# A shorter formula for g when h is small, with the long one in a second program behind a bound

## Chip, core and metric

The kernel runs on one NeuronCore of a Trainium2 chip. The metric is the device time of one execution in microseconds (us); the lower the better. Names of engines: PE is TensorE (matmuls), ACT is ScalarE, DVE is VectorE, POOL is GpSimd, SP is SyncE, which issues most DMAs.

## What is computed

Attention with a sigmoid in place of the softmax, and behind it a two-layer product with the function h - tanh(h) between the layers. Shapes: 8 batches, 12 heads, 448 tokens, 64 columns a head; the layers are 768 x 2048 and 2048 x 768.

```python
scores = scale * np.matmul(q, k.transpose(0, 1, 3, 2)) - np.log(S)
attn = 1.0 / (1.0 + np.exp(-scores))
x = np.matmul(attn, v)            # then (B*S, H*D)
h = x @ w_in
g = h - np.tanh(h)
out = g @ w_out
```

With the reference's own inputs h is small: its largest magnitude is 0.0230, worked out from them.

## The kernel before

All work goes batch by batch, 448 tokens each. A batch has an attention part (scores, `weigh` for the sigmoid, `split_a`, `av`), a first product `moe1` (x by w_in, into `ph`) and a second, `moe2` (g by w_out, into `po`, and `por` for the last 64 tokens). Numbers that need more than 16 bits are split into a high and a low half of 16 bits (`parts`, `split`, `halves`), and a product then takes three matmuls. While PE does the second product of batch b, ACT and DVE do the attention of batch b + 1, whose matmuls stand among those of the product; so PE has one unbroken queue. In batch 0 there is no batch before it: there the weights are loaded and split among the rest, and the first product is done in 32 bits (line 999 of the page).

`mix` makes g from h. It is called once for each pair of 128 columns of h, 8 times a batch, 64 times in all, on a tile of 128 partitions x 896 values (two halves of 448 tokens). Before, it computes two things: a polynomial m in u = h² (two Squares with biases on ACT, two products on DVE), good for small h, and th = h - tanh(h) (Tanh on ACT, one subtraction on DVE), good for large h. A Relu of u - 0.65² on ACT is zero or not, and `copy_predicated` on DVE (line 845) puts th in place of m where it isn't. `halves` splits the result into the two 16-bit halves of `g`, one on ACT (line 780) and one on DVE (line 781), a pair later (`finish_g`).

The order on PE, ACT, DVE and POOL is the order in which the code is written (`manual_schedule`). In batch 0 a string, `ORDER`, spells it out, letter by letter: `M` is half a pair of the first product, `t` the next step of the generator `mix`, `P` a step of the second product, `B` a block of the attention of batch 1, `A` and `a` a split of w_out, `C` a step of the loading of w_out. A `t` whose generator has ended does nothing. In the batches after it, `mix` runs behind each pair in `moe1`; its last call of a batch is carried out during the second product, at the steps named in `TAIL` (1, 2, 3, 4, 5), where a step is six matmuls of 384 columns.

Four kinds of PSUM tiles are shared: `sc` (two buffers: scores, `ph`), `mm` (two: `po`), `av` and `tr` (one each: sums of the attention, transposes). A matmul into one waits until the last reader of the tile before has ended. So `mix` holds `ph` until the last of its instructions that reads it.

Of the kernel before, what the change touches and what calls it, by code (L numbers as in the profile page):

```python
# [10 lines left out]
F32 = mybir.dt.float32  # L11
# [3 lines left out]
AF = mybir.ActivationFunctionType  # L15
ALU = mybir.AluOpType
AX = mybir.AxisListType
PSUM = bass.MemoryType.PSUM

P = 128  # L20
# [4 lines left out]
CUT = 0.65  # L25

KAPPA = 0.00592396
B1, C1 = 0.62576354, 2.54375998**2  # L30
# [1 line left out]


class Builder:

    AV32 = 2

# [23 lines left out]
    def __init__(self, ctx, tc, q, k, v, w_in, w_out, out):  # L61
        self.tc, self.nc = tc, tc.nc
        self.q, self.k, self.v, self.w_in, self.w_out, self.out = q, k, v, w_in, w_out, out
        self.B, self.NP, _, self.S = q.shape
        self.DM, self.DFF = w_in.shape
        self.NC = self.DM // P
        self.NF = self.DFF // P
        self.HALF = self.DM // 2
        nc = self.nc
        pool = lambda name, bufs, **kw: ctx.enter_context(tc.tile_pool(name=name, bufs=bufs, **kw))  # L70
        self.const = pool("const", 1)
        self.wp = pool("weights", 1)
        self.sm = pool("small", 2)
        self.nat = pool("nat", 2)
        self.qk = pool("qk", 2)
        self.att = pool("att", 2)
        self.xp = pool("xp", 8)
        self.tp = pool("temps", self.TP)
        self.op = pool("outs", 2)
        self.ps = pool("ps", 1, space=PSUM)  # L80

        self.ident = self.const.tile([P, P], F32, name="ident")
        make_identity(nc, self.ident)
        self.rows = self.const.tile([P, D], BF16, name="rows")
        nc.vector.tensor_tensor(self.rows, self.ident[:, 0::2], self.ident[:, 1::2], op=ALU.add)
        self.onesf = self.const.tile([P, P], F32, name="onesf")
        nc.vector.memset(self.onesf, 1.0)
        self.onesb = self.const.tile([P, P], BF16, name="onesb")
        nc.vector.memset(self.onesb, 1.0)

        self.NB = self.DFF // 256
        self.wi = self.wp.tile([P, self.NC * self.NB + self.SHIFT, 2, 256], F16, name="wi")
        self.wo = self.wp.tile([P, self.NF * 2 + self.SHIFT_O, 2, self.HALF], F16, name="wo")
# [628 lines left out]
    def h_scales(self, ix):  # L722

        V = self.nc.vector
        t1 = lambda name: self.sm.tile([P, 1], F32, name=name)
        ih, ihk = t1("ih"), t1("ihk")
        V.tensor_tensor(ih, ix, self.iSwi, op=ALU.mult)
        V.tensor_scalar(ihk, ih, KAPPA, None, op0=ALU.mult)
        return ih, ihk

    def split_x(self, hl, x, Sx, act):
# [89 lines left out]
    def mix(self, ps, g, ih, ihk):  # L821

        nc = self.nc
        V = nc.vector
        temp = lambda name: self.tp.tile([P, 2, self.S], F32, name=name, tag="t")
        u = temp("u")
        nc.scalar.activation(u, ps, AF.Square, scale=ih)  # L827
        th = temp("th")
        nc.scalar.activation(th, ps, AF.Tanh, scale=ih)  # L829
        m = temp("m")  # L830
        V.scalar_tensor_tensor(m, ps, ihk, u, op0=ALU.mult, op1=ALU.mult)  # L831
        V.scalar_tensor_tensor(th, ps, ih, th, op0=ALU.mult, op1=ALU.subtract)  # L832
        yield 1
        self.finish_g()
        yield 1
        q1 = temp("q1")
        nc.scalar.activation(q1, u, AF.Square, bias=self.b1)  # L837
        V.scalar_tensor_tensor(m, q1, C1, m, op0=ALU.add, op1=ALU.mult)  # L838
        yield 1
        q2 = temp("q2")  # L840
        nc.scalar.activation(q2, u, AF.Square, bias=self.b2)  # L841
        V.scalar_tensor_tensor(m, q2, C2, m, op0=ALU.add, op1=ALU.mult)  # L842
        yield 1
        nc.scalar.activation(u, u, AF.Relu, bias=self.b3)  # L844
        V.copy_predicated(m, u.bitcast(U32), th)  # L845
        yield 1
        self.late.append((m, g))
# [88 lines left out]
    def build(self):  # L936
        nc, tc = self.nc, self.tc

        def const(name, value, n=1):
            t = self.const.tile([P, n], F32, name=name)  # L940
            nc.vector.memset(t, value)
            return t

        self.nls = const("nls", -math.log(self.S))
        self.b1 = const("b1", B1)
        self.b2 = const("b2", B2)
        self.b3 = const("b3", -CUT * CUT)
        self.tiny = const("tiny", TINY)
        self.ih0 = const("ih0", 1.0)
        self.ihk0 = const("ihk0", KAPPA)  # L950
        self.iSwo = const("iswo", 1.0, 3)
        self.sums = [const(f"ss{i}", 0.0, 6) for i in range(2)]
        self.Swo = []
        self.sums_out, self.bound = [[], []], [None, None]
        self.xs32, self.x2b = False, []
        pieces = list(self.pieces())
        nA = 4 * self.NC
        E = mybir.EngineType
        with tc.manual_schedule(engines={E.PE, E.Activation, E.DVE, E.Pool}):
            nB = nA + self.NF + self.EARLY  # L960
            self.stage = tc.alloc_tile_pool(name="stage", bufs=2, reuse_waits="tile")
            self.blocks = self.stream()
            self.first(
                self.convert(pieces[:nA], "attention"),
                self.convert(pieces[nA:nB], "mixture"),
                self.convert(pieces[nB:], "product"),
            )
        with tc.manual_schedule(engines={E.PE, E.Activation, E.DVE, E.Pool, E.SP}):
            for b in range(1, self.B):
                self.batch(b)  # L970
        self.gp.release()
# [148 lines left out]
        assert not events  # L1120


def build_kernel(tc, q, k, v, moe_w_in, moe_w_out, out):
    with ExitStack() as ctx:
        Builder(ctx, tc, q, k, v, moe_w_in, moe_w_out, out).build()


# [27 lines left out]
```

## Time and profile before

| | |
|---|---|
| device time, median of 3 runs | 1165.98 us (1165.82 to 1166.71) |
| profiled execution, span from first to last instruction | 1164.3 us |
| PE, busy with matmuls | 1152.6 us, 99% of the span, 7585 matmuls |
| DVE | 904.5 us, 78% |
| ACT | 863.5 us, 74% |
| POOL | 77.9 us, 7% |
| PE's granted clock | 0.999 of full speed |

Of the profiled execution the page tells its span and no other time; the median lies 1.7 us over it, which is what stands around the first and last instruction. An engine's share is an average over stages. What one stage is worth is read from the stretches, and from what an engine waited for in each. The records of PE's matmuls overlap, since they are pipelined: a record is longer than the distance from one to the next.

### The profile page before, as it was taken

The page shows a single profiled execution, that of the slowest core. Times are in us where ns is not written, and L with a number is a line of the kernel's source. Part 1 is how long each engine was busy: PE and PEld are TensorE (multiplying, and loading weights), DVE is VectorE, ACT ScalarE, POOL GpSimd, SP SyncE. Part 2 cuts the span into 40 slices and gives each one's busy share as a digit, 9 for nine tenths or more (in the row PEclk, how much of TensorE's full clock was granted, in tenths as well). Part 3 has the DMA queues.
Part 4 walks back from the last instruction along what each step waited for, and adds up shares of the span by engine and source line. Part 5 has one row for each costly group of instructions (what it writes and reads, how often), then busy time and mean ns, then how long its engine had stood idle before and what let it go on. Part 6 is the DMA issues. An engine that isn't in the chain of part 4 may idle for free.

```text
span 1164.3 us, 18920 instructions
## 1 busy us (share of the span) xinstructions
PE 1152.6 (99%) x7585; PEld 601.2 (52%) x7585; DVE 904.5 (78%) x1294; ACT 863.5 (74%) x1185; POOL 77.9 (7%) x58
## 2 busy tenths in 40 slices
PE   9999999999999999999999999999999999999998
PEld 2355444555555555555555555555555555555565
DVE  6999998699866996679857897778976798646930
ACT  7998986589976888768887688867887688745820
POOL 0000000000220002100021000300022000300000
PEclk9999999999999999999999999999999999999999
DMA  9942171000321002210022100210012100000000
GB/s 358 360 161 72 45 219 54 22 8 1 88 78 60 1 1 77 62 53 1 17 75 62 40 1 31 87 58 19 1 60 80 53 1 10 22 28 8 1 15 34
DMA packets 34056, 70.43 MB, mean 60 GB/s; under 512 B 3888, under 2 KB 21040, under 8 KB 33968
## 3 DMA queue, kind: packets, MB, share of 16 engines
q1 hardware_dynamic: 33744, 68.89, 18.1%
q8 instruction: 59, 0.97, 0.3%
q10 hardware_dynamic: 224, 0.33, 0.1%
q14 instruction: 29, 0.24, 0.1%
HBM read 58.20 MB, written 11.01 MB: 59 GB/s over the span
## 4 chain that ended last, share of the span: by engine, by line
PE 88%; DVE 5%; ACT 3%; DMA 3%; issue 1%; DVEq 0%; ACTq 0%; SPq 0%
PE ph L787 33%; PE po L873 30%; PE acc L434 8%; PE sc L403 8%; PE por L921 5%; PE ph L999 3%; DMA raw<-moe_w_in 2%; DVE wo L250 1%; ACT a L414 1%; DMA qnn<-q 1%; DVE g L781 0%; DVE wo L249 0%; PE nm L704 0%; DVE m L845 0%; PE wl L204 0%
## 5 line engine op out<-in xcount | busy, mean ns | idle before, releaser
L873 PE MATMUL po<-wo,g 128*128 128x384 f16 x2304 | 388.7, 326 | 1.9 <-DVE wo L250 1.0
L787 PE MATMUL ph<-xhl,wi 128*128 128x448 f16 x2016 | 382.6, 352 | 0.0
L873 PEld LDWEIGHTS <-g 128*128 128x128 f16 x2304 | 220.6, 98 | 167.1 <-issue 23.5
L787 PEld LDWEIGHTS <-wi 128*128 128x128 f16 x2016 | 196.7, 98 | 185.0 <-issue 2.1
L421 DVE SCALAR_TENSOR_TENSOR ahl<-a,ahl 128x896 f16<-128x896 f32 x126 | 161.5, 1317 | 127.0 <-ACT ahl L420 126.9
L414 ACT ACTIVATE a<-sc,nls,rn 128x896 f32<-128x896 f32 x147 | 155.8, 1090 | 40.8 <-PE sc L403 39.4
L827 ACT ACTIVATE u<-ph,ih 128x896 f32<-128x896 f32 x64 | 64.4, 1006 | 72.3 <-PE ph L787 70.7
L420 ACT ACTIVATE ahl<-a 128x896 f16<-128x896 f32 x126 | 113.2, 940 | 0.6
L403 PE MATMUL sc<-Q,K 64*128 64x448 f16 x1008 | 100.8, 353 | 2.0 <-DVE th L832 1.3
L780 ACT ACTIVATE g<-m,Sg 128x896 f16<-128x896 f32 x64 | 66.6, 1041 | 36.6 <-DVE m L845 30.3
L831 DVE SCALAR_TENSOR_TENSOR m<-ph,ihk,u 128x896 f32<-128x896 f32 x64 | 73.4, 1147 | 24.1 <-ACT th L829 23.8
L845 DVE COPY_PREDICATED m<-u,th 128x896 f32<-128x896 uint32 x64 | 77.3, 1208 | 7.1 <-ACT u L844 0.8
L434 PE MATMUL acc<-ahl,vhl 128*64 128x448 f16 (+1 forms) x864 | 80.6, 356 | 0.0
L781 DVE SCALAR_TENSOR_TENSOR g<-m,Sg,g 128x896 f16<-128x896 f32 x64 | 73.3, 1146 | 6.7 <-ACT g L780 6.7
L465 POOL TENSOR_TENSOR x<-x 128x448 f32<-128x448 f32 x24 | 27.1, 1128 | 763.9 <-ACT x L448 763.9
L842 DVE SCALAR_TENSOR_TENSOR m<-q,m 128x896 f32<-128x896 f32 x64 | 69.8, 1091 | 6.8 <-DVE m L838 0.5
L999 PE MATMUL ph<-x,wi 128*128 128x448 f32 x192 | 74.1, 540 | 0.0
L832 DVE SCALAR_TENSOR_TENSOR th<-ph,ih,th 128x896 f32<-128x896 f32 x64 | 73.2, 1144 | 0.0
L838 DVE SCALAR_TENSOR_TENSOR m<-q,m 128x896 f32<-128x896 f32 x64 | 69.5, 1086 | 0.0
L844 ACT ACTIVATE u<-u,b 128x896 f32<-128x896 f32 x64 | 66.7, 1042 | 1.9
L837 ACT ACTIVATE q<-u,b 128x896 f32<-128x896 f32 x64 | 65.8, 1028 | 0.0
L841 ACT ACTIVATE q<-u,b 128x896 f32<-128x896 f32 x64 | 65.8, 1028 | 0.0
(142 smaller groups left out, 1086.3 us busy)
## 6 DMA issues: line engine op xcount, KB each, us to landing
knn<-k SPq DMA_DIRECT2D x45, 224.0 KB, 2.6
qnn<-q SPq DMA_DIRECT2D x44, 224.0 KB, 2.6
rawo<-moe_w_out SPq DMA_DIRECT2D x22, 384.0 KB, 5.6
out<-o SPq DMA_DIRECT2D x21, 384.0 KB, 2.3
raw<-moe_w_in SPq DMA_DIRECT2D x13, 512.0 KB, 8.1
vn<-v SPq DMA_DIRECT2D x24, 256.0 KB, 2.8
wo<-moe_w_in SPq DMA_DIRECT2D x11, 512.0 KB, 8.3
vn<-v SPq DMA_DIRECT2D x24, 192.0 KB, 2.4
```

What stands on the lines that cost most here:

```text
L403: self.nc.tensor.matmul(ps[i * m : (i + 1) * m, h, : self.S], K[i][r, w, c * P : c * P + m], Q[i][r, x, :], start=(n == 0), stop=(n == len ...
L414: self.nc.scalar.activation(a[:, 0], ps[:, :, : self.S], AF.Sigmoid, bias=self.nls, scale=scale)
L420: nc.scalar.activation(A[:, 0], a[:, 0], AF.Copy, scale=A_SCALE)
L421: nc.vector.scalar_tensor_tensor(A[:, 1], a[:, 0], A_SCALE, A[:, 0], op0=ALU.mult, op1=ALU.subtract)
L434: self.nc.tensor.matmul(acc[i][h * D : (h + 1) * D, : self.S], v[k, w, 2 * QT + h if half else h * QT + c], A[k, x, h], start=(n == 0 and ...
L781: nc.vector.scalar_tensor_tensor(g[:, 1], m, Sg, g[:, 0], op0=ALU.mult, op1=ALU.subtract)
L787: self.nc.tensor.matmul(ph, self.wi[:, self.slot(c, k), part, e * P : (e + 1) * P], xhl[c][:, x, :], start=(i == 0), stop=(i == len(prods) ...
L831: V.scalar_tensor_tensor(m, ps, ihk, u, op0=ALU.mult, op1=ALU.mult)
L832: V.scalar_tensor_tensor(th, ps, ih, th, op0=ALU.mult, op1=ALU.subtract)
L845: V.copy_predicated(m, u.bitcast(U32), th)
L873: nc.tensor.matmul(po[i][:, :H], gs[f // 2][:, x, f % 2, tk * P : (tk + 1) * P], self.wo[:, i * self.NF + 2 * ks[f // 2] + f % 2, w], star ...
L999: nc.tensor.matmul(ph[:, e, :S], self.fp32(self.wi, self.slot(c, k))[:, 0, e * P : (e + 1) * P], xs[c], start=(c == 0), stop=(c == self.NC ...
```

## The change

A class `Small` takes the place of `Builder`, with another `mix`. It has the polynomial alone, of one degree less: u = h² (ACT), m = h·u·κ (DVE), one Square with a bias (ACT), one product (DVE); no tanh, no Relu, no predicated copy, and three steps in place of five. A `tensor_reduce` keeps the largest u of each partition in one column of `squares` for each pair. After the last pair of the last batch, `largest` reduces these columns, transposes them on PE and reduces again, to one number in `flag`. Behind the whole program each engine loads the flag into a register and compares it with 0x3D7FFFFF (the bits of the float just under 0.0625, that is |h| = 0.25). Above it, the kernel of before runs, complete, and writes the output again.

```diff
+SMALL_BITS = 0x3D7FFFFF
+KAPPA_S = 0.051974997
+B_S, C_S = -1.2822222, 4.7692432
...
-        V.tensor_scalar(ihk, ih, KAPPA, None, op0=ALU.mult)
+        V.tensor_scalar(ihk, ih, self.KAPPA, None, op0=ALU.mult)
...
+class Small(Builder):
+    KAPPA = KAPPA_S
+
+    def __init__(self, ctx, tc, flag, *args):
+        super().__init__(ctx, tc, *args)
+        V = self.nc.vector
+        self.flag = flag
+        self.squares = self.const.tile([P, self.B * self.NB], F32, name="squares")
+        V.memset(self.squares, 0.0)
+        self.bs = self.const.tile([P, 1], F32, name="bs")
+        V.memset(self.bs, B_S)
+        self.seen = 0
+
+    def mix(self, ps, g, ih, ihk):
+        nc = self.nc
+        V = nc.vector
+        temp = lambda name: self.tp.tile([P, 2, self.S], F32, name=name, tag="t")
+        u = temp("u")
+        n, self.seen = self.seen, self.seen + 1
+        nc.scalar.activation(u, ps, AF.Square, scale=ih)
+        m = temp("m")
+        V.scalar_tensor_tensor(m, ps, ihk, u, op0=ALU.mult, op1=ALU.mult)
+        yield 1
+        self.finish_g()
+        yield 1
+        q = temp("q")
+        nc.scalar.activation(q, u, AF.Square, bias=self.bs)
+        V.scalar_tensor_tensor(m, q, C_S, m, op0=ALU.add, op1=ALU.mult)
+        V.tensor_reduce(self.squares[:, n : n + 1], u, axis=AX.XY, op=ALU.max)
+        if self.seen == self.B * self.NB:
+            self.largest()
+        yield 1
+        self.late.append((m, g))
+
+    def largest(self):
+        nc = self.nc
+        m = self.sm.tile([P, 1], F32, name="largest")
+        nc.vector.tensor_reduce(m, self.squares, axis=AX.X, op=ALU.max)
+        pt = self.ps.tile([P, 512], F32, name="lt", tag="tr", bufs=1)
+        nc.tensor.transpose(pt[:1, :P], m, self.ident)
+        nc.vector.tensor_reduce(self.flag, pt[:1, :P], axis=AX.X, op=ALU.max)
+
+def build_kernel(tc, *args):
+    nc = tc.nc
+    with tc.tile_pool(name="flag", bufs=1) as pool:
+        flag = pool.tile([1, 1], F32, name="flag")
+        with ExitStack() as ctx:
+            Small(ctx, tc, flag, *args).build()
+        bits = nc.values_load(
+            flag.bitcast(mybir.dt.int32), skip_runtime_bounds_check_because="it is compared, nothing else"
+        )
+        with tc.If(bits > SMALL_BITS):
+            with ExitStack() as ctx:
+                Builder(ctx, tc, *args).build()
```

How it moves the instructions, at three places. The rows name line, operation and tiles; in brackets stand the semaphores that a row waits for (of an engine, or of a DMA queue, DMAHW). In after the lines stand seven further down (781 is 788, 250 is 257), and `mix` is at 1152 to 1161.

DVE at the last pair of batch 0, among the splits of w_out (`wo`), before:

```order
L845 COPY_PREDICATED m<-u,th 128x896 [waits DVE_49,Activation_49]
L831 SCALAR_TENSOR_TENSOR m<-ph,ihk_110,u 128x896 [waits PE_49,Activation_49]
L832 SCALAR_TENSOR_TENSOR th<-ph,ih_108,th 128x896
L250 SCALAR_TENSOR_TENSOR wo<-wo,swo_s 128x2x384 [waits Activation_49]
L781 SCALAR_TENSOR_TENSOR g<-m,Sg,g 128x896 [waits Activation_49]
L859 TENSOR_SCALAR iK<-iswo,iSg 128x1
L838 SCALAR_TENSOR_TENSOR m<-q_1096,m 128x896 [waits DVE_49,Activation_49]
L249 TENSOR_SCALAR wo<-wo,swo_s 128x2x384 [waits DVE_49]
L250 SCALAR_TENSOR_TENSOR wo<-wo,swo_s 128x2x384 [waits DVE_49]
L842 SCALAR_TENSOR_TENSOR m<-q_1137,m 128x896 [waits Activation_49]
L296 TENSOR_REDUCE mo<-wl 128x1 [waits PE_49]
L845 COPY_PREDICATED m<-u,th 128x896 [waits DVE_49,Activation_49]
```

The same place in after, from the reduction of the pair before on:

```order
L1161 TENSOR_REDUCE squares<-u 128x1
L257 SCALAR_TENSOR_TENSOR wo<-wo,swo_s 128x2x384 [waits Activation_49]
L1154 SCALAR_TENSOR_TENSOR m<-ph,ihk_118,u 128x896 [waits Activation_49]
L257 SCALAR_TENSOR_TENSOR wo<-wo,swo_s 128x2x384 [waits Activation_49]
L788 SCALAR_TENSOR_TENSOR g<-m,Sg,g 128x896 [waits Activation_49]
L866 TENSOR_SCALAR iK<-iswo,iSg 128x1
L1160 SCALAR_TENSOR_TENSOR m<-q,m 128x896 [waits DVE_49,Activation_49]
L1161 TENSOR_REDUCE squares<-u 128x1
L256 TENSOR_SCALAR wo<-wo,swo_s 128x2x384 [waits DVE_49]
L257 SCALAR_TENSOR_TENSOR wo<-wo,swo_s 128x2x384 [waits DVE_49]
L303 TENSOR_REDUCE mo<-wl 128x1 [waits PE_49]
```

The tanh half, the second product and the predicated copy are gone from between the splits of w_out, a reduction has come in, and the splits and the halves of `g` stay in their order.

DVE at the last pair of the last batch, up to the evacuation `o` of the second product, before:

```order
L831 SCALAR_TENSOR_TENSOR m<-ph,ihk,u 128x896 [waits PE_49,Activation_49]
L832 SCALAR_TENSOR_TENSOR th<-ph,ih,th 128x896
L859 TENSOR_SCALAR iK<-iswo,iSg 128x3
L781 SCALAR_TENSOR_TENSOR g<-m,Sg,g 128x896 [waits Activation_49]
L838 SCALAR_TENSOR_TENSOR m<-q_11670,m 128x896 [waits DVE_49,Activation_49]
L842 SCALAR_TENSOR_TENSOR m<-q_11679,m 128x896 [waits DVE_49,Activation_49]
L845 COPY_PREDICATED m<-u,th 128x896 [waits DVE_49,Activation_49]
```

And in after:

```order
L1154 SCALAR_TENSOR_TENSOR m<-ph,ihk,u 128x896 [waits Activation_49]
L866 TENSOR_SCALAR iK<-iswo,iSg 128x3
L788 SCALAR_TENSOR_TENSOR g<-m,Sg,g 128x896 [waits Activation_49]
L1160 SCALAR_TENSOR_TENSOR m<-q,m 128x896 [waits DVE_49,Activation_49]
L1161 TENSOR_REDUCE squares<-u 128x1
L1171 TENSOR_REDUCE largest<-squares 128x1 [waits DVE_49]
L1174 TENSOR_REDUCE flag<-lt 1x1 [waits PE_49]
```

Between `largest` and `flag` there is now a row of PE (`lt`). In PE's queue it stands behind 12 matmuls of the last second product, the first two steps of 48 (buffer numbers are kept here):

```order
L880 MATMUL po1_11219<-wo_101,g_10860 128x384
L1173 MATMUL lt_11240<-ident_89,largest_11238 1x128 [waits DVE_49]
L880 LDWEIGHTS g_10923 [waits Activation_49]
L880 MATMUL po0_11218<-wo_101,g_10923 128x384
L880 LDWEIGHTS g_10923
```

PE had no row there that waits for DVE; else its order is that of before to the last matmul.

ACT at the end of the program, before:

```order
L906 ACTIVATE o<-po_11654,iK 128x384 [waits DMAHW3_49,PE_49]
L906 ACTIVATE o<-po,iK 128x384 [waits DMAHW4_49,DMAHW5_49,DMAHW2_49,PE_49]
L906 ACTIVATE o<-po_11869,iK 128x384 [waits DVE_49,DMAHW6_49,PE_49,Activation_49]
L866 DMA out<-orem 64x384 [waits DVE_49]
L1151 UNCONDITIONAL_BRANCH
```

And in after, where the last two rows are the first of the second program:

```order
L913 ACTIVATE o<-po_11434,iK 128x384 [waits DVE_49,DMAHW6_49,PE_49,Activation_49]
L873 DMA out<-orem 64x384 [waits DVE_49]
L1183 TENSOR_LOAD flag [waits DVE_49]
L1186 COMPARE_AND_BRANCH
L334 DMA qnn<-q 128x448 [waits Activation_49]
L680 ACTIVATE one<-nls 128x1 [waits DVE_49,PE_49]
```

A load of the flag and a jump have come in behind the last DMA, on this engine and likewise on the four others. Where the flag is small the jump goes over the second program, 1,066 rows on ACT, to the common end.

## Rows read from the trace of the kernel before

**Rows 1.** Busy time of each engine in three stretches: the first product of batch 0, the rest of batch 0, all behind it. Columns: stretch, its length, then busy time and number of instructions of PE, weight loads (PEld), DVE, ACT and POOL, PE's granted clock, share and rate of the DMAs.

```profile
50.12:128.23 78.11, 78.11 (x228) 39.16 (x228) 75.95 (x124) 67.63 (x106) 0.00 (x0) 1.00 0.33 113
128.23:225.56 97.33, 92.75 (x660) 45.35 (x659) 81.89 (x138) 72.83 (x120) 5.40 (x4) 1.00 0.33 101
225.56:1160.24 934.68, 934.66 (x6466) 501.91 (x6466) 707.47 (x955) 682.22 (x902) 71.78 (x48) 1.00 0.12 35
```

**Rows 2.** Groups of instructions of the whole span, those of `mix` on DVE and ACT: line, engine, operation, tiles, shapes, count, busy us, mean ns of one, idle time before them and what ended it.

```profile
L845 DVE COPY_PREDICATED m<-u,th 128x896 f32<-128x896 uint32 x64 | 77.3, 1208 | 7.1 <-ACT u L844 0.8 <-ACT u L827 0.5
...
L832 DVE SCALAR_TENSOR_TENSOR th<-ph,ih,th 128x896 f32<-128x896 f32 x64 | 73.2, 1144 | 0.0
L842 DVE SCALAR_TENSOR_TENSOR m<-q,m 128x896 f32<-128x896 f32 x64 | 69.8, 1091 | 6.8 <-DVE m L838 0.5
L838 DVE SCALAR_TENSOR_TENSOR m<-q,m 128x896 f32<-128x896 f32 x64 | 69.5, 1086 | 0.0
...
L844 ACT ACTIVATE u<-u,b 128x896 f32<-128x896 f32 x64 | 66.7, 1042 | 1.9
...
L841 ACT ACTIVATE q<-u,b 128x896 f32<-128x896 f32 x64 | 65.8, 1028 | 0.0
...
L829 ACT ACTIVATE th<-ph,ih 128x896 f32<-128x896 f32 x64 | 64.0, 1000 | 0.0
```

**Rows 3.** Timeline of PE from 124 to 230 us, six rows before which it waited and one more (`pbn`). Columns: start, length, line, operation, tiles, shapes, count, idle time before and what ended it.

```profile
133.43 0.74 PE L403 MATMUL sc<-Q,K 64*128 64x448 f16 x6 [1.27 <-DVE th L832]
...
141.42 0.39 PE L353 MATMUL pbn<-ss,onesf 128*128 128x4 f32 x2
...
147.78 0.32 PE L873 MATMUL po<-wo,g 128*128 128x384 f16 x1 [0.43 <-DVE wo L250]
148.85 0.82 PE L873 MATMUL po<-wo,g 128*128 128x384 f16 x4 [0.74 <-DVE g L781]
...
160.12 0.39 PE L353 MATMUL pbn<-ss,onesf 128*128 128x4 f32 x2 [0.71 <-ACT sqn L345]
...
190.18 0.74 PE L403 MATMUL sc<-Q,K 64*128 64x448 f16 x6 [0.73 <-ACT a L414]
...
196.93 6.82 PE L873 MATMUL po<-wo,g 128*128 128x384 f16 x41 [0.57 <-DVE wo L250]
```

**Rows 4.** Timeline of DVE in the same stretch, with the same columns.

```profile
131.17 1.14 DVE L831 SCALAR_TENSOR_TENSOR m<-ph,ihk,u 128x896 f32<-128x896 f32 x1
132.22 1.15 DVE L832 SCALAR_TENSOR_TENSOR th<-ph,ih,th 128x896 f32<-128x896 f32 x1
...
143.52 0.16 DVE L359 TENSOR_TENSOR un<-tn 128x2 f32<-128x2 f32 x1 [0.40 <-ACT tn L355]
...
146.71 1.02 DVE L250 SCALAR_TENSOR_TENSOR wo<-wo,swo_s 128x768 f16<-128x768 f32 x1
147.65 1.14 DVE L781 SCALAR_TENSOR_TENSOR g<-m,Sg,g 128x896 f16<-128x896 f32 x1
```

**Rows 5.** Timeline of ACT in the same stretch, with the same columns.

```profile
128.82 0.99 ACT L827 ACTIVATE u<-ph,ih 128x896 f32<-128x896 f32 x1
...
142.17 0.55 ACT L446 ACTIVATE x<-acc 128x448 f32<-128x448 f32 x1
...
143.24 0.25 ACT L355 ACTIVATE tn<-pbn,tiny 128x4 f32<-128x4 f32 x1
```

**Rows 6.** Timelines of PE, ACT and DVE where the last batch goes from the first product to the second, with the same columns.

```profile
1105.34 12.84 PE L873 MATMUL po<-wo,g 128*128 128x384 f16 x78
...
1105.54 1.01 ACT L827 ACTIVATE u<-ph,ih 128x896 f32<-128x896 f32 x1 [0.87 <-PE ph L787]
...
1107.48 1.15 DVE L831 SCALAR_TENSOR_TENSOR m<-ph,ihk,u 128x896 f32<-128x896 f32 x1
1108.55 1.14 DVE L832 SCALAR_TENSOR_TENSOR th<-ph,ih,th 128x896 f32<-128x896 f32 x1
...
1109.73 1.14 DVE L781 SCALAR_TENSOR_TENSOR g<-m,Sg,g 128x896 f16<-128x896 f32 x1
1110.80 1.08 DVE L838 SCALAR_TENSOR_TENSOR m<-q,m 128x896 f32<-128x896 f32 x1
```

**Rows 7.** The end, from several views: the timeline (last matmuls, last DMA issue of ACT), the list of DMA issues (count, size, median us from issue to landing), the stretch 1162 to 1163 (columns as in rows 1), the DMA queue that fetches instructions (packets, MB, share of 16 engines' time) and, from the start of the timeline, a load of ACT's tables.

```profile
1157.78 2.44 PE L921 MATMUL por<-wo,g 128*64 128x384 f16 x28
...
1160.92 0.55 ACTq L866 DMA_DIRECT2D out<-orem  x1
...
out<-orem ACTq DMA_DIRECT2D x1, 96.0 KB, 2.4
...
1162.00:1163.00 1.00, 0.00 (x0) 0.00 (x0) 0.00 (x0) 0.00 (x0) 0.00 (x0) 0.72 0.76 197
...
q8 instruction: 59, 0.97, 0.3%
...
1.18 1.28 ACT L673 ACT_TABLE_LOAD   x1 [1.18 <-PEq L1133]
```

**Rows 8.** Instructions by tile, those that reduce along a row on DVE and the one transpose on PE: line, engine, operation, count, duration in ns (least, median, most), first and last start, shapes.

```profile
L706 DVE TENSOR_REDUCE m<-nm x8: 615/617/625, 57.0 to 1041.1; 128x1 f32<-128x448 f32 x8
...
L279 DVE TENSOR_REDUCE st<-cn x1: 680/680/680, 62.9 to 62.9; 128x1 f32<-128x512 f32 x1
...
L282 PE MATMUL pt<-ident,st x1: 270/270/270, 67.0 to 67.0; 128*1 128x128 f32 x1
```

More of the change, by code (lines that the diff above doesn't have):

```diff
@@ L34 @@
 class Builder:
+    KAPPA = KAPPA
     AV32 = 2
@@ L949, in build @@
         self.ih0 = const("ih0", 1.0)
-        self.ihk0 = const("ihk0", KAPPA)
+        self.ihk0 = const("ihk0", self.KAPPA)
         self.iSwo = const("iswo", 1.0, 3)
@@ L1120, in second @@
         assert not events
-def build_kernel(tc, q, k, v, moe_w_in, moe_w_out, out):
-    with ExitStack() as ctx:
-        Builder(ctx, tc, q, k, v, moe_w_in, moe_w_out, out).build()
+class Small(Builder):
[48 more added lines that the diff above has]
+                Builder(ctx, tc, *args).build()
 def kernel(q, k, v, moe_w_in, moe_w_out):
@@ L1151 @@
     with tile.TileContext(nc) as tc:
-        build_kernel(tc, **args)
+        build_kernel(tc, *(args[n] for n in ("q", "k", "v", "moe_w_in", "moe_w_out", "out")))
     r = run_bass_kernel_spmd(nc, [arrays], core_ids=[0])
```

## The prediction

> **What bounds the kernel now.** I read three views in this order. First the busy time by stretch [rows 1]: from 50.12 to 128.23 us PE is busy for 78.11 of 78.11 us, from 225.56 to 1160.24 for 934.66 of 934.68, and only between them, 128.23 to 225.56, does it stand for 97.33 - 92.75 = 4.58 us. So the kernel is PE's own work, and what the change takes off DVE and ACT can be worth time in that one stretch alone, the second product of batch 0. Second, the groups of instructions in `mix` [rows 2], for what is removed. Third, the timelines: where PE does wait [rows 3 to 5], where the last batch goes from the first product to the second [rows 6], and the end of the program [rows 7].
>
> In PE's rows a matmul is longer than its issue distance: 78 products take 12.84 us, 0.165 us each, while the record of a single one is 0.32 us [rows 3, 6]. So each wait is some 0.16 us longer than the idle time shown. With six waits [rows 3] the stretch holds about 4.6 + 1.0 = 5.6 us. That is the ceiling of any gain.
>
> **What is removed and added in `mix`.** Per pair DVE loses L832, L842 and L845 (1.14 + 1.09 + 1.21 = 3.44 us) and gains a reduction of 128x896; ACT loses Tanh, one Square and the Relu (1.00 + 1.03 + 1.04 = 3.07 us) [rows 2]. The trace has no reduction of that size. Two of its form took 617 ns for 448 elements and 680 ns for 512 [rows 8], 0.98 ns an element on a base of 0.18 us: an estimate of 1.06 us for 896. So 64 times 2.4 us leave DVE and 64 times 3.1 us leave ACT, some 350 us in all. In batches 1 to 7 this is worth nothing: it all lies beside a PE that waits for 0.02 us in 934.68. What remains of `mix` is of kinds that stand in rows 2 (L838, L841).
>
> **Batch 0, where DVE is late.** PE's scores at 133.43 waited for DVE's L832 to release `ph`, which ended at 132.22 + 1.15 = 133.37 [rows 3, 4]. L832 is gone, and the last reader of `ph` is `m`. DVE began that at 131.17 although ACT's `u` was there at 128.82 + 0.99 = 129.81 [rows 4, 5]: DVE had a backlog of removed instructions. Without it, `m` ends near 129.8 + 1.2 = 131.0, before PE asks at 133.43 - 1.27 = 132.2: the first wait goes, 1.3 us.
>
> From there PE's attention sums and `pbn` (141.42) come 1.3 us earlier, at 140.1. ACT evacuated those sums (`x`) only at 142.17, behind a Relu that is gone; now it does it when PE has them, at about 140.1, and `tn` follows 143.24 - 142.17 = 1.07 us later [rows 5], at 141.2: 2.1 us earlier. DVE's chain from `un` at 143.52 over the split at 146.71 to `g` at 147.65 has no removed instruction in it and hangs on `tn` [rows 4]; it moves by the same 2.1 us, and so does PE's restart at 148.85, which waits for that `g`. The later waits (160.12, 190.18, 196.93) [rows 3] end the same chain of conversions and splits, with nothing of `mix` in it: they move and don't shrink. **Gain 2.1 us**; ends 1.3 (the first wait alone) and 5.6 (all six). I take 2.1 since the order behind `tn` is unchanged.
>
> **Batch 7, a new wait of PE.** The transpose `lt` waits for DVE, and 276 products and the 96 matmuls of `por` are queued behind it. PE reaches it 12 matmuls into the second product, at 1105.34 + 12 x 0.165 = 1107.3 [rows 6]. DVE gets there later: ACT's `u` ends at 1105.54 + 1.01 = 1106.55; `m` starts at 1106.6; iK and `g` 1.18 us behind it (as 1108.55 to 1109.73), the second `m` another 1.07 (1109.73 to 1110.80) and the reduction another 1.07, at 1109.9 [rows 6]. It takes 1.06 us, to 1111.0; the 128x64 reduction, on the same line, 0.18 + 0.06 = 0.24; the transpose 0.27 [rows 8]. PE goes on at about 1111.4: **4.1 us lost**, and nothing behind it makes that up, for PE has no other idle time there. Ends: 3.4 and 4.8, each of five handovers 0.14 us shorter or longer.
>
> The clock can fall in that wait. PE's last matmul ended at 1157.78 + 2.44 = 1160.2, and from 1162 to 1163 the granted clock was 0.72 on average [rows 7]: it went from 1.0 (2.4 GHz) to 0.5 (1.2 GHz) near 1162.4, 2.2 us behind PE's last work. A wait of 4.1 us is longer. No row shows how soon it rises again. I take as long at half speed as it took to fall, 2.2 us, of which half is lost: **1.1 us**; ends 0 (no fall) and 2.1 (a slow stretch as long as the wait).
>
> **The end, a load and a jump on every engine.** On ACT the load needs only the flag, set 50 us earlier, so it starts when the DMA issue before it ends, 1160.92 + 0.55 = 1161.47. That DMA lands at 1160.92 + 2.4 = 1163.3, and the end waits for it [rows 7]: 1.85 us of cover. The trace shows neither such a load nor a jump over a thousand rows. Nearest are ACT's table load, 1.28 us; and for the fetch of instructions at the target, on the low side the mean packet of the instruction queue (0.3% of 16 engines over 1164.3 us for 59 packets, 0.95 us), on the high side the 2.4 us of a small DMA from issue to landing [rows 7]. Lower end: both inside the cover, 0. Middle: 1.28 + 2.4 - 1.85 = 1.8. Upper: a second fetch, for the common end, 1.8 + 2.4 = 4.2. I take the middle: a fetch that nothing foresaw pays the whole way of a DMA, not the packet alone. **1.8 us.**
>
> Here the Trainium skill speaks against the change: "Runtime: NRT & Kernel Launch", section Instruction fetch mechanics, says that a taken branch whose target isn't among the pages held forces a fetch of the target's page before the engine goes on. No row of before shows such a jump; without that rule the end would cost 0 and the sum below would be 3.1 us. "DMA: Bandwidth & Descriptors", section Latency and other measured facts, gives a floor of some 600 ns for a tensor_load, which no row shows either; by it the end would cost 1.1 us and the sum would be 4.2.
>
> **The sum.** -2.1 + 4.1 + 1.1 + 1.8 = +4.9 us. The span of the profiled execution, 1164.3 us, becomes 1169.2; what lies around it, 1165.98 - 1164.3 = 1.7 us by the median, stays: **1170.9 us**, 0.4% slower. A measurement of this kernel can tell about 0.2%, 2.3 us, from no change.
>
> **The rivals.** *All of batch 0's waits go.* If ACT, lighter by 3.1 us a pair, and the temporaries that `mix` no longer takes (three of the shared pool instead of five) let the later loads start earlier, the chain behind 148.85 gains too: -5.6 + 4.1 + 1.1 + 1.8 = +1.4, 1167.4 us, not slower. For it: DVE or ACT ends all six waits. Against: from 143.52 on DVE has no removed work. It decides from a gain of 4.7 us upward. Chance 0.12.
> *The clock holds and the jump is hidden*: -2.1 + 4.1 = +2.0, 1168.0 us, within 0.2%. For it: the cover of 1.85 us. Against: the fall after 2.2 us. 0.12.
> *Two fetches and a long fall*: -2.1 + 4.1 + 2.1 + 4.2 = +8.3, 1174.3 us. For it: two jumps stand at the end, to the other branch and to the common end; against: these two lie side by side. 0.12.
> *The short formula isn't enough and the second program runs*: near 2 x 1165, 2,330 us. The largest |h| of the reference's inputs is 0.0230, its square 0.00053, against a bound of 0.0625: 0.01.
> *A gain*: all six waits gone, no fall, a hidden jump and a transpose under 3 us, below 1163.6: 0.03.
>
> **How the numbers follow.** The forecast has the rest, 0.60, with 1168.4 to 1173.4 of its own. Slower: 0.60 + 0.12 + 0.01 = 0.73. Within 0.2%: 0.24. Faster: 0.03. The range leaves out the gain, the lower half of the first rival, the upper third of the long one and the second program, under 0.2 in all: 1167.3 to 1174.6.
>
> **What the profile will show.** Right: PE's idle time from 128 to 226 us down by about 2, with the wait at 133.43 gone; one wait of some 4 us of PE on DVE two steps into the last second product, and a granted clock of 0.5 for a stretch behind it; from the last matmul to the end of the span some 1.8 us more than 1164.3 - 1160.2 = 4.1; batches 1 to 6 the same. Wrong: idle time of PE in those batches; a reduction far over 1.06 us, which lengthens the new wait by as much; a clock that stays at 1.0; or a far smaller distance at the end.

## The result

The changed kernel takes 1173.84 us (median of 4 runs, 1173.52 to 1173.98), the kernel before, in the same runs, 1166.33 us. The ratio is 1.0065, 95% interval 1.0051 to 1.0079: 7.5 us slower, where 4.9 were forecast. The second program doesn't run: PE's matmuls are those of one program and the transpose, 7586. The span of the profiled execution is 1171.5 us against 1164.3, 7.2 us more. Profiles also differ in how long the kernel's start takes: over all of them the first `po` of batch 0 starts between 127.51 and 129.62 us. So I go by stretches of the traces where I can. The 7.2 us stand at three places.

**Batch 0.** PE's timeline of the changed kernel, with the columns of [rows 3]: the first product of `po`, the four waits that are left, and the first product of batch 1.

```profile
128.09 2.11 PE L880 MATMUL po<-wo,g 128*128 128x384 f16 x12
...
146.62 0.82 PE L880 MATMUL po<-wo,g 128*128 128x384 f16 x4 [0.69 <-DVE g L788]
...
157.90 0.38 PE L360 MATMUL pbn<-ss,onesf 128*128 128x4 f32 x2 [0.72 <-ACT sqn L352]
...
187.96 0.74 PE L410 MATMUL sc<-Q,K 64*128 64x448 f16 x6 [0.73 <-ACT a L421]
...
194.71 6.82 PE L880 MATMUL po<-wo,g 128*128 128x384 f16 x41 [0.57 <-DVE wo L257]
...
223.27 6.98 PE L794 MATMUL ph<-xhl,wi 128*128 128x448 f16 x36
```

The waits at 133.43 and 147.78 of [rows 3] are gone, the four others stand with nearly their old lengths, 2.2 us earlier each. The step is set by PE's restart behind `g`: 146.62 - 128.09 = 18.53 us behind the first `po`, before 148.85 - 128.23 = 20.62. From the first `po` to the first `ph` PE takes 223.27 - 128.09 = 95.18 us; before it was 225.49 - 128.23 = 97.26. Gain 2.1 us. The row of before for this, and the first `por` of the last batch, before and after, for the next place:

```profile
225.49 4.71 PE L787 MATMUL ph<-xhl,wi 128*128 128x448 f16 x24
```

```profile
1152.23 7.99 PE L921 MATMUL por<-wo,g 128*64 128x384 f16 x96
```

```profile
1155.67 7.99 PE L928 MATMUL por<-wo,g 128*64 128x384 f16 x96
```

I use this stretch and the restart below. In the other profiles with the short formula and no added work (e1 to e8) the stretch takes 95.0 to 95.4 us.

**Batch 7.** Timelines of PE, ACT and DVE of the changed kernel where the last batch goes to its second product.

```profile
1103.06 2.11 PE L880 MATMUL po<-wo,g 128*128 128x384 f16 x12
1108.94 0.27 PE L1173 MATMUL lt<-ident,largest 128*1 128x128 f32 x1 [3.77 <-DVE largest L1171]
1109.05 16.14 PE L880 MATMUL po<-wo,g 128*128 128x384 f16 x88
...
1103.26 1.01 ACT L1152 ACTIVATE u<-ph,ih 128x896 f32<-128x896 f32 x1 [3.94 <-PE ph L794]
...
1104.30 1.15 DVE L1154 SCALAR_TENSOR_TENSOR m<-ph,ihk,u 128x896 f32<-128x896 f32 x1 [2.60 <-ACT u L1152]
...
1105.49 1.14 DVE L788 SCALAR_TENSOR_TENSOR g<-m,Sg,g 128x896 f16<-128x896 f32 x1
1106.56 1.08 DVE L1160 SCALAR_TENSOR_TENSOR m<-q,m 128x896 f32<-128x896 f32 x1
1107.56 1.08 DVE L1161 TENSOR_REDUCE squares<-u 128x1 f32<-128x896 f32 x1
1108.67 0.22 DVE L1171 TENSOR_REDUCE largest<-squares 128x1 f32<-128x64 f32 x1
```

DVE's chain is the predicted one, instruction by instruction. PE comes to the transpose at 1103.06 + 1.98 = 1105.04 and goes on at 1109.05: 4.0 us. PE's granted clock, in the column behind the five engines:

```profile
1108.00:1109.00 1.00, 0.06 (x1) 0.06 (x2) 0.85 (x2) 0.72 (x1) 0.00 (x0) 1.00 0.00 0
1109.00:1110.00 1.00, 1.00 (x5) 0.56 (x6) 0.75 (x2) 0.00 (x0) 0.00 (x0) 0.59 0.00 0
1110.00:1111.00 1.00, 1.00 (x5) 0.49 (x4) 0.59 (x1) 0.00 (x0) 0.00 (x0) 0.50 0.00 0
1111.00:1112.00 1.00, 1.00 (x5) 0.46 (x3) 0.00 (x0) 0.00 (x0) 0.00 (x0) 0.50 0.00 0
1112.00:1113.00 1.00, 1.00 (x6) 0.50 (x4) 0.00 (x0) 0.00 (x0) 0.00 (x0) 0.70 0.00 0
1113.00:1114.00 1.00, 1.00 (x9) 0.60 (x7) 0.00 (x0) 0.00 (x0) 0.00 (x0) 1.00 0.00 0
```

It falls to half, 1.2 GHz, just when PE starts again, and stays there until about 1112.6. The missing parts of the four rows, 0.41 + 0.50 + 0.50 + 0.30, are 1.7 us of lost work. PE's busy column shows nothing of it; the count of matmuls in each us does, 5 instead of 8 or 9. From the first `po` to the first `por` it was 1152.23 - 1105.34 = 46.9 us before and is 1155.67 - 1103.06 = 52.6 us: 5.7 us, 4.0 of wait and 1.7 of clock. The same wait stands in e3, e5 and e6, and there this distance is 52.5 to 52.6 us too. The moment of the fall varies: in e5 PE was at work again from 1109.83, and the clock fell only at 1110.9; the slow stretch was 3.4 us long all the same.

**The end.** From the last matmul to the end of the span it was 4.1 us and is 1171.5 - 1163.7 = 7.8: 3.7 us more. The sequencers' instructions on two lines of the changed kernel, the load of the flag and the comparison with what follows (engine, operation, count, ns, start):

```profile
L1183 SPq TENSOR_LOAD <-flag x1: 958/958/958, 1164.9 to 1164.9; - x1
L1183 ACTq TENSOR_LOAD <-flag x1: 1068/1068/1068, 1164.9 to 1164.9; - x1
...
L1186 SPq EVENT_SEMAPHORE  x8: 17/17/17, 1169.6 to 1170.1; - x8
L1186 POOLq COMPARE_BRANCH  x1: 45/45/45, 1110.1 to 1110.1; - x1
L1186 POOLq EVENT_SEMAPHORE  x1: 17/17/17, 1110.3 to 1110.3; - x1
L1186 PEldq COMPARE_BRANCH  x1: 3532/3532/3532, 1162.3 to 1162.3; - x1
L1186 DVEq COMPARE_BRANCH  x1: 72/72/72, 1164.3 to 1164.3; - x1
L1186 SPq COMPARE_BRANCH  x1: 50/50/50, 1165.9 to 1165.9; - x1
...
L1186 ACTq COMPARE_BRANCH  x1: 54/54/54, 1166.1 to 1166.1; - x1
L1186 DVEq EVENT_SEMAPHORE  x1: 21/21/21, 1167.2 to 1167.2; - x1
L1186 ACTq EVENT_SEMAPHORE  x1: 17/17/17, 1169.6 to 1169.6; - x1
```

The comparison takes 0.05 us on SP and ACT and 0.07 on DVE; the next instruction comes 3.5 us after its start on ACT, 3.7 on SP, 2.9 on DVE; on PE the comparison itself lasts 3.5. On POOL the same jump took 0.2 us; there it goes over a short program (the page of before counts 58 instructions on POOL, 1185 on ACT). The last DMA (issued 1164.36, 2.6 us to landing in this run) is there at 1167.0, 2.6 us before SP and ACT go on. The span ends 1.9 us behind SP's first instruction after the jump (1169.6 to 1171.5), and so it does in e1, e2 and e8.

Between these places nothing changed: from 225.56 to 1100 us PE is busy for 874.44 of 874.44 us in both kernels, though DVE has 570.06 us of work there instead of 690.55 and ACT 511.55 instead of 668.99.

### The profile page after: what moved, and what is told of

Same layout as the page of the kernel before. It is cut to its first block, busy times and chain, and to the rows that moved or that the text cites. A ratio compares the mean times of both kernels' runs of the same rounds, so it can differ in the third digit from the quotient of the medians.

```text
span 1171.5 us, 18358 instructions
## 1 busy us (share of the span) xinstructions
PE 1154.7 (99%) x7586; PEld 601.8 (51%) x7586; DVE 761.6 (65%) x1170; ACT 678.0 (58%) x993; POOL 77.8 (7%) x58
## 4 chain that ended last, share of the span: by engine, by line
PE 92%; DVE 3%; DMA 3%; ACT 1%; issue 0%; SPq 0%; DVEq 0%; ACTq 0%
PE ph L794 33%; PE po L880 30%; PE acc L441 8%; PE sc L410 8%; PE ph L1006 6%; PE por L928 5%; DMA raw<-moe_w_in 1%; DVE wo L257 1%; DMA vn<-v 1%; DMA wo<-moe_w_in 1%; PE wl L211 0%; DVE wo L256 0%; PE nm L711 0%; PE pbn L360 0%; DVE stb L190 0%
## 5 line engine op out<-in xcount | busy, mean ns | idle before, releaser
L1160 DVE SCALAR_TENSOR_TENSOR m<-q,m 128x896 f32<-128x896 f32 x64 | 69.4, 1084 | 0.9
L1161 DVE TENSOR_REDUCE squares<-u 128x1 f32<-128x896 f32 x64 | 69.0, 1078 | 0.0
L1159 ACT ACTIVATE q<-u,bs 128x896 f32<-128x896 f32 x64 | 66.0, 1031 | 0.3
L928 PE MATMUL por<-wo,g 128*64 128x384 f16 x768 | 64.9, 327 | 0.0
L410 PEld LDWEIGHTS <-K 64*128 64x128 f16 x1008 | 35.5, 97 | 52.4 <-issue 30.9
L441 PEld LDWEIGHTS <-vhl 128*64 128x64 f16 (+1 forms) x864 | 38.3, 108 | 40.2 <-issue 19.8
L928 PEld LDWEIGHTS <-g 128*64 128x64 f16 x768 | 42.4, 110 | 22.1 <-issue 4.5
```

Source lines behind the costliest of these rows:

```text
L410: self.nc.tensor.matmul(ps[i * m : (i + 1) * m, h, : self.S], K[i][r, w, c * P : c * P + m], Q[i][r, x, :], start=(n == 0), stop=(n == len ...
L441: self.nc.tensor.matmul(acc[i][h * D : (h + 1) * D, : self.S], v[k, w, 2 * QT + h if half else h * QT + c], A[k, x, h], start=(n == 0 and ...
L928: nc.tensor.matmul(po[e * D : (e + 1) * D, :H], gs[f // 2][:, x, f % 2, nm:S], self.wo[:, e * self.NF + 2 * ks[f // 2] + f % 2, w], start= ...
L1160: V.scalar_tensor_tensor(m, q, C_S, m, op0=ALU.add, op1=ALU.mult)
```

## The experiments

Times are medians, ratios are to the kernel before on the same chip (1166.04 us beside e1 to e4, 1166.38 beside e5 to e8). What a run gives back is told from times over that kernel, since the chips differ: the changed kernel is 7.5 us over it. The kernels without a second program (all but e1, e2 and e8) leave out the long formula for an h above the bound, except e7, which keeps it in batches 1 to 7.

**e1_late.** The transpose later in PE's queue.

```diff
-        if self.seen == self.B * self.NB:
-            self.largest()
...
+        if b + 1 == self.B and isinstance(self, Small):
+            events.append((24, self.largest))
         events.sort(key=lambda e: e[0])
```

> The transpose of `largest` stands 24 steps into the last second product instead of 2, all else as in the changed kernel. Theory (PE's wait for it and the slow clock behind it cost 5.7 us, from 46.9 us for the same 288 matmuls before to 52.6 after): 1173.8 - 5.7 = 1168.1 us, PE without a wait there and a granted clock of 1.0 throughout. Rival (the wait is of DVE's late chain and only moves, or the load of the flag becomes late): no change, 1173.8 us.

1167.86 us, ratio 1.0013 (1.0004 to 1.0022). PE's timeline of e1 has no wait at the transpose, and its matmuls run at 0.163 us each before and after it:

```profile
1102.72 23.56 PE L880 MATMUL po<-wo,g 128*128 128x384 f16 x144
1126.12 0.27 PE L1173 MATMUL lt<-ident,largest 128*1 128x128 f32 x1
1126.22 23.56 PE L880 MATMUL po<-wo,g 128*128 128x384 f16 x144
```

It is 1.8 us over the kernel before, so 5.7 us of the 7.5 came from where the transpose stood, as the theory has it; the rival falls.

**e2_fill.** PE works while it waits.

```diff
+        wt = self.ps.tile([P, 512], F32, name="fill", tag="av", bufs=1)
+        for _ in range(16):
+            nc.tensor.matmul(wt[:, :], self.onesb, self.onesb[:, None, :].to_broadcast([P, 4, P]), start=True, stop=True)
         nc.tensor.transpose(pt[:1, :P], m, self.ident)
```

> 16 matmuls of 512 columns that nobody uses fill PE's wait ahead of the transpose (about 3.5 of its 4 us); the transpose itself comes no earlier. Theory (the clock falls because PE stands, and costs 1.7 us behind the wait): granted clock 1.0 in the whole stretch and 1173.8 - 1.7 = 1172.1 us. Rival (the fall costs nothing, the matmuls are held by something else): 1173.8 us or more.

1171.63 us, 1.0046 (1.0032 to 1.0059): 5.6 us over the kernel before, 1.9 less than the changed kernel. The transpose is as late as ever (1109.21, 5.9 us behind the first `po`, as in the changed kernel), but the clock holds:

```profile
1109.00:1110.00 1.00, 0.79 (x6) 0.51 (x7) 0.64 (x3) 0.00 (x0) 0.00 (x0) 1.00 0.00 0
1110.00:1111.00 1.00, 1.00 (x8) 0.61 (x7) 0.86 (x1) 0.00 (x0) 0.00 (x0) 1.00 0.08 16
```

From the first `po` to the first `por` it is 50.9 us instead of 52.6, the 1.7 of the clock. So useless matmuls made the kernel faster: the clock's part is real, and it comes of PE standing.

**e3_no_if.** The flag is computed, the load, branch and second program are left out.

```diff
-        bits = nc.values_load(
-            flag.bitcast(mybir.dt.int32), skip_runtime_bounds_check_because="it is compared, nothing else"
-        )
-        with tc.If(bits > SMALL_BITS):
-            with ExitStack() as ctx:
-                Builder(ctx, tc, *args).build()
```

> The flag is computed as in the changed kernel, but no engine loads it and there is no branch and no second program. Theory (load and jump cost 3.7 us at the end): 1173.8 - 3.7 = 1170.1 us, and 4.1 us from the last matmul to the end of the span. Rival (the longer distance at the end comes of something else, such as slower last DMAs): 1173.8 us.

1170.19 us, 1.0032 (1.0020 to 1.0045). From the last matmul (1165.1) to the end (1169.2) 4.1 us, as before the change: load and jump are the 3.7 us of the trace, and the theory holds. The median is 4.2 us over the kernel before, so 3.4 less than the changed kernel, but it is loose: the six runs lie between 1167.9 and 1171.9, and in the profiled one the granted clock was also at 0.50 from 28.2 to 31.7 us.

**e4_plain.** As e3, and the reductions and `largest` are left out too (their lines in `mix` removed).

> Only the short formula: no reductions, no `largest`, no load, no branch. Theory (the lighter mix is worth 2.2 us in batch 0 and nothing in the other batches): 1166.2 - 2.2 = 1164.0 us, PE's idle time from 128 to 226 us down by about 2 us. Rival (without the 64 reductions DVE is still further ahead and more of the six waits goes): up to 5.6 us, 1160.6 us.

1164.34 us, 0.9985 (0.9976 to 0.9994). The stretch of batch 0 takes 95.19 us, as with the reductions (95.18): the reductions of 1.08 us cost nothing there. Only the last of the 64 costs something in the changed kernel, as a part of the wait for the transpose. This kernel is 1.7 us faster than the one before, but it has no guard, and its formula is good for small h alone.

**e5_load_only.** As e3, with `values_load` kept.

> As e3_no_if (flag computed, no second program, no branch), but every engine loads the flag into a register at the end. Theory (of the 3.7 us at the end the load's 1.0 us lies under the last DMA's landing, the jump is what shows): as e3_no_if, 1170.2 us. Rival (the load stands in the open): 1171.2 us.

1170.95 us, 1.0039 (1.0023 to 1.0054). It tells nothing of the load: as nothing uses the register, the program has no load in it, and its trace shows only the waits for the flag. It is a second e3, and shows how far two such medians can lie apart.

**e6_near_branch.** The branch goes over one instruction.

```diff
         with tc.If(bits > SMALL_BITS):
-            with ExitStack() as ctx:
-                Builder(ctx, tc, *args).build()
+            nc.vector.memset(flag, 0.0)
```

> Load, comparison and branch as in the changed kernel, but the branch goes over one memset instead of the whole second program (above the bound the long formula is left out). Theory (the 3.5 us behind the comparison are the fetch of a far target): 1170.2 us plus under 1 us for the added waits at the end, 1170.2 to 1171.2. Rival (any branch that is taken costs this, or the register's way to the comparison does): 1173.8 us.

1170.35 us, 1.0035 (1.0023 to 1.0047), as e3. On SP and ACT the scheduler put the branch ahead of the last DMAs here, so these two don't count; DVE and PE have it behind their last work, as in the changed kernel:

```profile
L1186 PEldq COMPARE_BRANCH  x1: 223/223/223, 1162.8 to 1162.8; - x1
L1186 DVEq COMPARE_BRANCH  x1: 72/72/72, 1164.8 to 1164.8; - x1
L1186 DVEq EVENT_SEMAPHORE  x1: 21/21/21, 1165.1 to 1165.1; - x1
```

0.2 us on PE instead of 3.5, 0.3 us from comparison to the next instruction on DVE instead of 2.9. What costs is the distance of the target, not the branch; the 0.2 us on POOL in the changed kernel say the same. That a far jump fetches instructions is seen in the two DMA queues that bring them (packets, MB, share), first the changed kernel, then e6:

```profile
q8 instruction: 61, 1.00, 0.4%
...
q14 instruction: 30, 0.25, 0.1%
```

```profile
q8 instruction: 59, 0.97, 0.3%
...
q14 instruction: 24, 0.20, 0.1%
```

From 1155 us to the end nine of these packets come in the changed kernel, one in e6 and one in e3.

**e7_batch0_only.** As e4, with the long `mix` from the ninth pair on.

```diff
+        n, self.seen = self.seen, self.seen + 1
+        if n >= self.NB:
+            yield from super().mix(ps, g, ih, ihk)
+            return
```

> The short formula in batch 0 alone (8 of 64 pairs), the long one in batches 1 to 7; no reductions, no flag, no branch. Theory (all of the gain is in batch 0): as e4_plain, 1164.3 us. Rival (the 56 other pairs give their share, by less contention or fewer late reads of PSUM): near 1166.0 us.

1164.44 us, 0.9981 (0.9972 to 0.9990), as e4. Eight pairs of 64 carry the whole gain; the 56 others are worth nothing that shows.

**e8_late_early_load.** As e1, and the flag is loaded at step 40.

```diff
+            events.append((40, self.load_flag))
...
+    def load_flag(self):
+        self.bits = self.nc.values_load(
+            self.flag.bitcast(mybir.dt.int32), skip_runtime_bounds_check_because="it is compared, nothing else"
+        )
```

> As e1_late (transpose 24 steps into the last second product), and the load of the flag on every engine stands at step 40 of 48 + 16 instead of the end; the branch stays at the end. Theory (ACT's load of 1.07 us stands ahead of the jump on the path to the end): 1167.9 - 1.0 = 1166.9 us. Rival (PE or another engine stops for the load in the middle): 1167.9 us or up to 0.5 us more.

1167.05 us, 1.0005 (0.9996 to 1.0014): with the guard no longer to be told from the kernel before. It is 0.7 us over that kernel where e1 is 1.8, but the two intervals overlap, so that the earlier load is worth 1 us is not shown. PE didn't stop for its load. The jump began earlier and took longer, 3.9 us on ACT here:

```profile
L1191 ACTq COMPARE_BRANCH  x1: 54/54/54, 1159.2 to 1159.2; - x1
...
L1191 ACTq EVENT_SEMAPHORE  x1: 17/17/17, 1163.1 to 1163.1; - x1
```

In e1 it was 3.2 us. On SP, which the end follows, the comparison came 0.5 us behind the start of the last DMA issue instead of 1.6, but the jump took 4.0 us instead of 2.6; from the last matmul to the end it is 7.1 us here and 6.8 in e1. Why the jump varies wasn't tried.

**e9_act_kept and e10_dve_kept.** Which engine's relief counts in batch 0. Each ran once, and so did e11. Both as e4 (the kernel of e9 has no reductions either, though its expectation names them).

```diff
+        th = temp("th")
+        nc.scalar.activation(th, ps, AF.Tanh, scale=ih)
...
+        nc.scalar.activation(q2, u, AF.Square, bias=self.b2)
...
+        nc.scalar.activation(u, u, AF.Relu, bias=self.b3)
```

```diff
+        V.scalar_tensor_tensor(th, ps, ih, u, op0=ALU.mult, op1=ALU.subtract)
...
+        V.scalar_tensor_tensor(q2, q, C_S, th, op0=ALU.add, op1=ALU.mult)
...
+        V.copy_predicated(q2, u.bitcast(U32), th)
```

> No load, no branch. The short formula and the reductions, with ACT's Tanh, second Square and Relu kept as work whose results nobody reads; DVE's three instructions are gone. From the first `po` of batch 0 to the first `ph` of batch 1 PE took 97.3 us before and 95.2 in the changed kernel. Theory (the first wait of 1.3 us is DVE's backlog, the further 0.8 us need the Relu out of ACT's way): 96.0 us. Rival (DVE's relief alone brings all of it): 95.2 us.

> No load, no branch, no reductions. The short formula, with a second read of `ph`, a second product and a predicated copy kept on DVE as work whose results nobody reads; ACT's three instructions are gone. Theory (DVE's backlog is what PE waits for at the first wait): the stretch that took 97.3 us before and 95.2 in the changed kernel takes 96.8 to 97.3 us. Rival (ACT's Tanh and Relu were the hold-up): 95.2 us.

1166.38 and 1167.23 us, the kernel before beside them 1167.5; single runs, so the stretch has to tell. It takes 97.55 us in e9 and 97.82 in e10, PE's restart comes 20.27 and 21.13 us behind the first `po` (20.62 before, 18.53 in the changed kernel and in e4). In e9 theory and rival both fall: with DVE relieved the first wait of 1.27 us goes, as I said (one of 0.24 for ACT comes behind it), but only 0.35 us of it arrives at the restart. And the stretch loses that again, by the clock. PE's rows of e9:

```profile
146.41 0.32 PE L880 MATMUL po<-wo,g 128*128 128x384 f16 x1 [0.16 <-DVE wo L256]
147.46 0.32 PE L880 MATMUL po<-wo,g 128*128 128x384 f16 x1 [0.73 <-DVE wo L257]
148.53 1.08 PE L880 MATMUL po<-wo,g 128*128 128x384 f16 x4 [0.74 <-DVE g L788]
149.54 2.42 PE L410 MATMUL sc<-Q,K 64*128 64x448 f16 x12
```

The twelve `sc` take 2.42 us instead of 1.31: the granted clock is 0.50 from 149.0 to 152.4, behind three waits that follow each other closely, none as long as 1 us. From the restart to the first `ph` it is 77.28 us instead of 76.64, so without the fall e9's stretch would be some 96.9 us (an estimate), still nearer to 97.3 than to the 96.0 of the theory. ACT's rows of e9 and of e4 show why the rest of the 1.3 us doesn't arrive:

```profile
138.94 1.05 ACT L1167 ACTIVATE u<-u,b 128x896 f32<-128x896 f32 x1
...
142.91 0.25 ACT L362 ACTIVATE tn<-pbn,tiny 128x4 f32<-128x4 f32 x1
```

```profile
138.03 2.08 ACT L421 ACTIVATE a<-sc,nls,rn 128x896 f32<-128x896 f32 x2
140.32 0.54 ACT L453 ACTIVATE x<-acc 128x448 f32<-128x448 f32 x1 [0.22 <-PE acc L441]
...
141.38 0.25 ACT L362 ACTIVATE tn<-pbn,tiny 128x4 f32<-128x4 f32 x1
```

With its old work ACT is busy through to `tn`, 142.91 - 128.26 = 14.65 us behind the first `po` (15.01 before); without it ACT waits for PE and `tn` comes at 141.38 - 128.47 = 12.91. In e10 it is DVE that holds `ph` (0.68 us at the first wait). There PE's scores at 140.37 also wait 1.22 us for ACT's `a`, and `tn` comes 15.51 us behind. That `a` starts at 139.23, just behind the second product that DVE keeps (138.02 + 1.08 = 139.10); whether it waited for it wasn't tried.

**e11_five_tiles.** Both kept kernels also take five tiles of the shared pool instead of three. e4 with two more tiles:

```diff
+        th = temp("th")
+        V.memset(th[:, 0, 0:1], 0.0)
...
+        q2 = temp("q2")
+        V.memset(q2[:, 0, 0:1], 0.0)
```

> As e4_plain, but `mix` takes five tiles of the shared pool again, as before the change, instead of three; each of the two extra ones gets a memset of one column and is read by nobody. Theory (ACT and DVE must both be lighter, the pool has no part): the stretch from the first `po` of batch 0 to the first `ph` of batch 1 is 95.2 us as in e4_plain, at most 0.2 more for the memsets. Rival (the tiles kept in e9 and e10, not the work on ACT and DVE, held things up): 97.3 us or more.

1164.96 us (the kernel before beside it 1167.34), the stretch 95.41 us, the restart at 18.53 us: taking five tiles alone costs nothing there. In e9 and e10 the two extra tiles are also held until kept work has ended; that part was not tried by itself.

## Why the prediction was right

The direction, the places and in the main the mechanisms held; of four terms, two were too small, and they missed on the same side: 1173.84 us is 2.9 us over the forecast of 1170.9, and nearer to the rival of two fetches and a long fall, 1174.3.

- **Nothing in batches 1 to 7**: shown by e7 and by PE's unchanged 874.44 us. The two lighter engines gave 120.5 + 157.4 us there, and none of it was on the path.
- **Gain in batch 0**: 2.1 us forecast, 2.1 measured (95.18 against 97.26). The step by which `tn` sets it, when ACT has the sums as soon as PE, is what the rows show. One bound was wrong: I gave 1.3 us for the first wait alone, as if it could be kept. In e9, with the first wait gone and ACT's work kept, 0.35 us reached PE's restart; the chain behind it takes back the rest unless ACT is lighter too.
- **The wait for the transpose**: 4.1 forecast, 4.0 measured; by e1 it cost that, with the clock's 1.7 behind it; the reduction took 1.08 us against an estimate of 1.06.
- **The clock**: 1.1 forecast, 1.7 measured (e2 gave that back with the filled wait). The mis-sized step is "as long at half speed as it took to fall, 2.2 us": the slow stretch lasted 3.4 us, 1109.2 to 1112.6, and the fall took 4.0 us from PE's last product (1105.2), not 2.2. So neither half of that step is shown: the 2.2 us came from one row, at the end of the program; at the same place it is 3.5 us in the changed kernel and 5.3 in e2. That a wait longer than those 2.2 us brings the fall is therefore not shown; that PE's standing brings it, e2 shows.
- **The end**: 1.8 forecast, 3.7 measured (in e3 it is gone). That the DMA's landing covers only a part of load and jump was right. The mis-sized step is the fetch at the whole way of a small DMA, 2.4 us: it took 3.5 on ACT and 3.7 on SP. The load took 1.07 us, near the 1.28 assumed. The rest is a term that I put at nothing: behind the jump SP runs 8 semaphore instructions of the branch and 10 of the common end, where the kernel before has 7 at its end in all, and from its first one to the end of the span it is 1.9 us, where before it was 1.0 from the last landing. I also followed ACT; the end follows SP. The rule of the Trainium skill ("Runtime: NRT & Kernel Launch", section Instruction fetch mechanics) is borne out by e6 against the changed kernel, 0.2 us to a near target and 3.5 to a far one on PE, and by the packets of the instruction queues. Why a far jump takes 2.6 us at one place and 4.0 at another stays open.

The sum of the measured terms, -2.1 + 4.0 + 1.7 + 3.7 = +7.3, is the 7.2 us of the spans. Of the rivals, the one in which all of batch 0's waits go fell (four of six stand), and the one in which the clock holds and the jump is hidden fell on both counts. The one with two fetches and a long fall is right in its sizes, a longer fall (1.7 of its 2.1 us) and an end of 3.7 of its 4.2; whether the one gap on each engine holds one fetch or several the traces don't tell. The second program didn't run, and a gain didn't come.

## What to carry to other kernels

Where one engine is busy without a gap, taking work from its neighbours (here a sixth of DVE's and a fifth of ACT's) is worth only what it waits for, and here both neighbours on the chain had to become lighter at once. What a guard adds must be placed by the busy engine's queue: one small instruction that depends on a slow engine cost 5.7 us at one place and nothing 22 steps later. A second program behind a branch that jumps it costs the fetch of a far target on four of the five engines here, even when it never runs; on POOL, with its short program, it cost 0.2 us.

## What was not expected of the hardware

A wait of 4.0 us of PE costs 1.7 us more behind it, in four traces, for the granted clock goes to half at about the time when PE starts again. In e9 it fell as well, behind three waits of 0.16 to 0.74 us in a row. A load of one word from SBUF into a register takes 0.47 to 0.54 us on all engines, but 0.96 us on SP and 1.07 us on ACT behind the last DMA issue (changed kernel; in e8, away from one, 0.52 and 0.47). A DMA issue just ahead isn't reason enough: in e6 SP's load starts 0.1 us behind one and takes 0.54 us. A far jump took 2.6 to 4.0 us in different places and runs.
